# A three-stage kernel (decayed attention, routing, two expert layers): logits, scan resets, first routing step and tail rearranged

## The chip, the cores and the metric

One core of one Trainium2 chip runs the whole program. The metric is the device time of one execution in microseconds. Before the change the median of three runs is 825.63 us (824.81 to 825.66). The engines are TensorE (PE, with its weight loads as PEld), VectorE (DVE), ScalarE (ACT), GpSimd (POOL) and SyncE (SP, here the main issuer of DMA). They run side by side and wait for each other through semaphores.

## The reference

```python
# 1: attention with a decaying state, B=4, H=8, S=768, D=48
f = 1.0 / (1.0 + np.exp(-f_logit))
for t in range(S):
    state = f[:, :, t, :, None] * state + np.einsum('bhd,bhe->bhde', k[:, :, t], v[:, :, t])
    y[:, :, t] = np.einsum('bhd,bhde->bhe', q[:, :, t], state)
# 2: y as x (3072 tokens x 384); each token goes to one of 8 experts, 384 tokens each:
#    all (token, expert) pairs by falling logit; a pair is taken if the token is free
#    and the expert not full
logits = x @ w_gate
out[mask] = np.maximum(x[mask] @ w1[e], 0.0) @ w2[e]
# 3: on the result, rows scaled by rms and rms_g
g = xn @ w_gate2
y = (g / (1 + np.exp(-g)) * (xn @ w_val)) @ w_out
```

## The kernel before

**Attention** (`attention`, lines 322 to 596). Sixteen units, each a batch and a pair of heads; four units make a batch. A unit's 768 positions are cut in 6 chunks of 128. For a unit, `decays` (L403) lets ScalarE make `G`, the sigmoid of the forget logits. `scans` (L424) resets `G` at each chunk's first position by a memset of a very large number on VectorE (L427), and then runs one scan forward (`P`, L428) and one back (`W`, L431). With `one`, a constant in PSUM, as the second operand, the reset starts the running product anew. `kt` (VectorE) and `qt` (GpSimd) are keys and queries times these. TensorE turns the keys (`k_back`, L455), makes the products of a chunk with itself (`inner`, L469) and the chunk sums `U` (L483), which VectorE scans into states `st` (L487). Two units later `values` (L503) makes the outputs into two PSUM banks, and ScalarE copies them to `YT` (L509; for the last unit VectorE copies one half). The units are written out in one order by the loop `for i in range(-1, NU + 2)`, with no scheduler behind it: each engine takes its instructions in written order.

**Logits.** After a batch's last `values`, `logits` (L515) multiplies `YT` with the gate weights, in four strips of the TensorE array, 32 output partitions each, one strip a pair of heads, for each half `g` of the positions. ScalarE copies the result out (`lgT`, L518). A little later `logits_turn` (L522) multiplies each 128 positions by `sel`, which adds the four strips up and turns them: six products of 8 columns a batch. ScalarE copies them to `lg` (L525).

**Routing** (`Route`, lines 79 to 260; `slots`, L273). While the last units run, VectorE takes the range of the first 18 of 24 blocks of 128 tokens (`range`, L113) and scales it (`start`, L127 to L180); this is `extra["edges"]` in the loop. Behind the last logits, `favourites` (L171) finds each token's best expert, `hits` (L75) compares its distance with 128 marks, and TensorE counts the tokens per mark and expert (`cnt`, L217). That is step 0; four more steps choose again among the open experts. Each step begins with some row blocks of `YT` that are turned back (`Rows.put`, L612), copied by ScalarE and stored to DRAM by SP (`Rows.take`, L621, L622). `slots` makes the list `idx` (L319), by which GpSimd gathers the rows for the experts (L842).

**Experts and the last layer.** Eight experts (L1088, L1089), then twelve chunks of the gated layer. At its end, behind the loop, the products of the last four of twelve blocks are made for the two outputs `O[0]` and `O[1]`, `finish` copies each (L1163), and GpSimd scatters it to DRAM (L1166).

Of the kernel before, what the change touches and what calls it, by code (L numbers as in the profile page):

```python
# [20 lines left out]
BIG = 1.0e30  # L21
# [49 lines left out]
def hits(nc, wk, name, marks, x, g, G):  # L71

    c = wk.tile([128, G // 4, 128, 4], BF, name=f"{name}{g}", bufs=1)
# [7 lines left out]
class Route:  # L81
# [9 lines left out]
    def __init__(self, tc, K, lg, A, ident, pmin, pool):  # L91
# [5 lines left out]
        self.m0 = pool.tile([128, NB], F32, name="m0")  # L97
        self.v = pool.tile([128, 3], F32, name="v")
# [8 lines left out]
        self.n = 0  # L107
# [59 lines left out]
    def favourites(self, oh, d):  # L167

        nc, NB, E, n = self.tc.nc, self.NB, self.E, self.n
        if n < NB:  # L170
            nc.vector.tensor_reduce(out=self.m0[:, n:], in_=self.lg[:, n:], axis=AX.X, op=OP.max)  # L171
        nc.vector.tensor_scalar(d, self.m0, self.gm[:, 2:3], self.s0, op0=OP.add, op1=OP.mult)
        nc.vector.tensor_tensor(out=oh, in0=self.lg, in1=self.m0[:, :, None].to_broadcast([128, NB, E]),
                                op=OP.is_equal)
# [8 lines left out]
    def steps(self, n, Tp, rows=None, side=None):  # L183
# [5 lines left out]
        with self.tc.tile_pool(name="r_wk", bufs=2) as wk, self.tc.tile_pool(name="r_ps", bufs=1, space=PSUM) as ps:  # L189
# [8 lines left out]
            def one(s):  # L198
                oh = wk.tile([128, NB, E], BF, name="oh")
                d = wk.tile([128, NB], BF, name="d")  # L200

                if rows:
                    for n in ((4,), (3, 2), (3, 2), (4,), (4,))[s]:
                        rows.put(n)
                        rows.take(n)
                    side(s)
# [5 lines left out]
                else:  # L212
                    self.favourites(oh, d)
                cnt = ps.tile([128, E], F32, name="cnt")
# [23 lines left out]
    def run(self, n, flag, idx, ident, rows=None, side=None, more=None):  # L238
# [4 lines left out]
        def check(wk, ps, cum):  # L243
# [4 lines left out]
            ct = ps.tile([128, E + 2], F32, name="ct")  # L248
# [25 lines left out]
def slots(tc, K, A, ident, idx, check=None):  # L274
# [3 lines left out]
    with tc.tile_pool(name="s_wk", bufs=1) as wk, tc.tile_pool(name="s_ps", bufs=1, space=PSUM) as ps:  # L278
# [30 lines left out]
        for g in range(0, NB, 8):  # L309
            hots.update(hits(nc, wk, "ro", K["io"], r, g, 8))  # L310
# [10 lines left out]

def attention(tc, fT, kT, qT, vL, YT, w_gate, lg, pmin, ident, gcol, rms_g, extra):

# [15 lines left out]

    NR = 3  # L340
# [32 lines left out]
    one = psl.tile([128, 1], F32, name="one")  # L373
# [6 lines left out]
    lgp = [t[:, 384:408].rearrange("p (n e) -> p n e", e=8) for t in YP]  # L380
    sel = cst.tile([128, 8], F32, name="sel")
# [4 lines left out]
    nc.vector.tensor_reduce(out=sel, in_=ident.rearrange("q (p e) -> q e p", p=NP)[:, 0:8, :], axis=AX.X, op=OP.add)  # L386
# [877 lines left out]
```

## Time and profile before

| what | us |
|---|---|
| median of the runs | 825.63 |
| the profiled execution, its own time | 826.22 |
| its span, first to last instruction | 824.5 |
| TensorE waits for `kt` of VectorE | at 15.58 (0.88) and 26.70 (0.69) |
| before the half-clock stretch from 28.8 | `values`, that wait, `k_back`, products of a unit |
| before the one from 49.3 | products of a unit, `U` sums (48 columns), a turn (8 columns) |
| one turn of logits, to the next product | 1.43 (95.20 to 96.63) |
| one row block turned back by TensorE | 0.42 (2.08 for 5, from 119.46) |
| one product into a last output | 0.18 (24 records from 812.75 to 817.08) |
| `idx` written, gathers start | 141.0, 142.2 |

The times are microseconds from the first instruction. A product of fp32 operands is two records of TensorE, and records overlap, so a group's mean duration is longer than its share of the busy time. The profiled execution is one of its own; its time is 0.6 us above the median of the runs.

### The profile page before, as it was taken

The numbers are of one execution on the slowest core, as the hardware profiler recorded it, in microseconds if no ns is written. First come the engines' busy times: TensorE is split into PE (matmuls) and PEld (weight loads), VectorE is DVE, ScalarE is ACT, GpSimd is POOL, SyncE is SP. The second block draws the span as 40 slices with busy tenths as digits, with TensorE's granted clock in tenths as the row PEclk, the third lists the DMA queues.
The fourth block names the chain that finished last, engine by engine and source line by source line (L and its number), as shares of the span: only waits on it lengthen the run. The fifth ranks groups of instructions, "written<-read, shape, count | busy, mean of one in ns | idle before, by whom it ended". The sixth has DMA issues, their size and how long they took to land.

```text
span 824.5 us, 16903 instructions
## 1 busy us (share of the span) xinstructions
PE 796.4 (97%) x6745; PEld 770.6 (93%) x6745; DVE 484.7 (59%) x868; ACT 387.9 (47%) x844; POOL 276.1 (33%) x328
## 2 busy tenths in 40 slices
PE   7999986999999999999999999999999999999996
PEld 7888875899999999999999999999999999999996
DVE  8999867778988988465443434434344434344322
ACT  5777653455554564675344342425343343424221
POOL 7878701277777787150201011010202010110100
PEclk9999997999999999999999999999999999999999
DMA  9997155877787779341000000000000000000000
GB/s 275 233 230 203 31 173 216 267 264 245 241 306 253 253 238 314 116 147 39 20 2 20 1 20 2 20 1 20 19 3 20 2 20 2 20 1 20 2 20 20
DMA packets 44246, 88.59 MB, mean 107 GB/s; under 512 B 5856, under 2 KB 23520, under 8 KB 44160
## 3 DMA queue, kind: packets, MB, share of 16 engines
q1 hardware_dynamic: 35088, 70.90, 27.7%
q0 software_dynamic: 3072, 9.44, 3.3%
q10 hardware_dynamic: 6000, 7.09, 2.5%
q8 instruction: 55, 0.90, 0.5%
q14 instruction: 31, 0.25, 0.1%
HBM read 70.90 MB, written 16.52 MB: 106 GB/s over the span
## 4 chain that ended last, share of the span: by engine, by line
PE 61%; issue 8%; DVE 8%; DMA 2%; ACT 2%; POOL 1%; ACTq 0%; DVEq 0%; POOLq 0%
PE o L630 5%; PE o L628 5%; PE o L629 5%; PE g L628 5%; PE g L630 5%; PE g L629 5%; PE v L630 5%; PE v L629 5%; PE v L628 5%; PE x L629 3%; PE x L630 2%; PE x L628 2%; DVE w L819 2%; PE h L629 2%; DVE nb L1012 2%
## 5 line engine op out<-in xcount | busy, mean ns | idle before, releaser
L1188 DVE TENSOR_TENSOR hf<-sg,v 128x256 f32<-128x256 f32 x144 | 59.9, 416 | 165.0 <-PE v L630 115.2
L950 POOL TENSOR_TENSOR xlo<-xn,xhi 128x256 fp32r<-128x256 f32 x36 | 29.4, 820 | 312.2 <-ACT xhi L949 312.2
L1191 ACT CAST hh<-hf 128x256 fp32r<-128x256 f32 x144 | 58.6, 407 | 132.4 <-DVE hf L1188 132.4
L630 PE MATMUL g<-xhi,w 128*128 128x256 f32 x432 | 119.3, 276 | 0.0
L628 PE MATMUL g<-xhi,w 128*128 128x256 f32 x432 | 119.3, 276 | 0.0
L629 PE MATMUL g<-xlo,w 128*128 128x256 f32 x432 | 119.3, 276 | 0.0
L630 PE MATMUL v<-xhi,w 128*128 128x256 f32 x432 | 119.3, 276 | 0.0
L628 PE MATMUL v<-xhi,w 128*128 128x256 f32 x432 | 119.2, 276 | 0.0
L629 PE MATMUL v<-xlo,w 128*128 128x256 f32 x432 | 119.2, 276 | 0.0
L1192 DVE TENSOR_TENSOR hl<-hf,hh 128x256 fp32r<-128x256 f32 x144 | 61.2, 425 | 68.1 <-ACT hh L1191 67.6
L630 PE MATMUL o<-w,hl 128*128 128x384 f32 x288 | 98.6, 342 | 0.0
L628 PE MATMUL o<-w,hh 128*128 128x384 f32 x288 | 97.4, 338 | 0.2 <-ACT hh L1191 0.2
L629 PE MATMUL o<-w,hh 128*128 128x384 f32 x288 | 97.1, 337 | 0.0
L1186 ACT ACTIVATE sg<-g 128x256 f32<-128x256 f32 x144 | 55.3, 384 | 88.2 <-PE g L630 87.9
L628 PEld LDWEIGHTS g<-xhi,w 128*128 128x128 f32 x432 | 81.1, 188 | 0.0
L629 PEld LDWEIGHTS v<-xlo,w 128*128 128x128 f32 x432 | 81.1, 188 | 0.0
L628 PEld LDWEIGHTS v<-xhi,w 128*128 128x128 f32 x432 | 81.1, 188 | 0.0
L630 PEld LDWEIGHTS v<-xhi,w 128*128 128x128 f32 x432 | 81.1, 188 | 0.0
L630 PEld LDWEIGHTS g<-xhi,w 128*128 128x128 f32 x432 | 81.1, 188 | 0.0
L629 PEld LDWEIGHTS g<-xlo,w 128*128 128x128 f32 x432 | 81.0, 188 | 0.0
L1015 POOL TENSOR_TENSOR nr<-nr,ne 128x384 f32<-128x384 f32 x36 | 61.4, 1705 | 43.2 <-DVE ne L1014 12.9
L629 PE MATMUL x<-hl,w 128*128 128x384 f32 x192 | 65.7, 342 | 3.4 <-DVE hl L1089 3.3
(237 smaller groups left out, 1880.8 us busy)
## 6 DMA issues: line engine op xcount, KB each, us to landing
wraw<-in_moe_w_dram SPq DMA_DIRECT2D x32, 768.0 KB, 7.7
v<-in_v_rows_dram SPq DMA_DIRECT2D x16, 288.0 KB, 4.7
x_dram<-xrows SPq DMA_DIRECT2D x24, 192.0 KB, 5.7
nraw<-in_moe_w_gate_dram SPq DMA_DIRECT2D x12, 384.0 KB, 4.6
nraw<-in_moe_w_val_dram SPq DMA_DIRECT2D x12, 384.0 KB, 3.9
nraw<-in_moe_w_out_dram SPq DMA_DIRECT2D x12, 384.0 KB, 4.1
raw_f<-in_f_logit_turned_dram SPq DMA_DIRECT2D x26, 144.0 KB, 5.4
raw_k<-in_k_turned_dram SPq DMA_DIRECT2D x26, 144.0 KB, 4.1
```

What stands on the lines that cost most here:

```text
L628: nc.tensor.matmul(out, lhs[0], rhs[0], start=first, stop=False)
L629: nc.tensor.matmul(out, lhs[0], rhs[1], start=False, stop=False)
L630: nc.tensor.matmul(out, lhs[1], rhs[0], start=False, stop=last)
L819: eng.tensor_tensor(out=lo, in0=raw, in1=hi.bitcast(F32), op=OP.subtract)
L950: eng.tensor_tensor(out=lo, in0=s, in1=hi.bitcast(F32), op=OP.subtract)
L1012: nc.vector.scalar_tensor_tensor(out=b, in0=hw, scalar=-0x40000000, in1=b, op0=OP.bitwise_and, op1=OP.bitwise_or)
L1015: nc.gpsimd.tensor_tensor(out=r, in0=r, in1=e2.bitcast(F32), op=OP.mult)
L1186: nc.scalar.activation(sg, pg, AF.Silu)
L1188: nc.vector.tensor_tensor(out=h, in0=sg, in1=pv, op=OP.mult)
L1191: nc.scalar.copy(hh, h)
L1192: nc.vector.tensor_tensor(out=hl, in0=h, in1=hh.bitcast(F32), op=OP.subtract)
```

## The change

- *Logits.* One PSUM bank a batch instead of two. A strip now holds three pieces of 128 positions in two columns' places (256 columns), and the four pairs of heads are added in PSUM by four rounds of products into the same strips. `sel` has two forms and the turn is two products of 48 columns. `sel` is now filled by ScalarE.
- *Scan resets.* A ScalarE copy of `big` behind the sigmoid replaces VectorE's memset, for all units but the first.
- *Early favourites.* For the first 16 blocks, favourites and comparisons are made ahead, behind `start`; they are counted by TensorE between the last logits and their turn. Step 0 has 8 blocks left. The counts, `one` and a check's sums lie in a PSUM bank of their own (`bank0`), and the comparisons in one fixed buffer (`cm`).
- *Order.* The memset of the banks for the last `values` stands before `start`; a minimum over `pall` stands later. Row blocks by step: 1, 2, 5, 5, 5, 6 instead of 2, 4, 5, 5, 4, 4 (the first number is ahead of the steps).
- *End.* The products for the last two outputs stand in another order, and the second output is copied in two halves, by ScalarE and VectorE.

```diff
+    def early(self, pool, cnt):
+        nc, NB, E = self.tc.nc, self.NB, self.E
+        n = self.ready = 16
+        self.cnt = cnt
+        self.oh0 = pool.tile([128, NB, E], BF, name="oh0")
+        self.d0 = pool.tile([128, NB], BF, name="d0")
+        self.favourites(self.oh0, self.d0, 0, n)
+        self.hot = {}
+        self.compare(0, 12)
+    def compare(self, g, G):
+        self.hot.update(hits(self.tc.nc, self.cm, "cm", self.K["io"], self.d0, g, G))
+    def count(self):
+        for i, c in self.hot.items():
+            self.tc.nc.tensor.matmul(self.cnt, c, self.oh0[:, i], start=(i == 0), stop=False)
...
-                    for n in ((4,), (3, 2), (3, 2), (4,), (4,))[s]:
+                    for n in ((2,), (3, 2), (3, 2), (3, 2), (3, 3))[s]:
...
-                for g, G in self.PARTS:
-                    for i, c in hits(nc, wk, "cm", K["ed"] if s else K["io"], d, g, G).items():
+                for g, G in ((16, 8),) if ahead else self.PARTS:
+                    for i, c in hits(nc, self.cm, "cm", K["ed"] if s else K["io"], d, g, G).items():
...
             nc.scalar.activation(G[i][:, t], raw("f", i)[:, t], AF.Sigmoid)
+        if i:
+            nc.scalar.copy(G[i][:, 0:S:C], big)
...
-        nc.vector.memset(g[:, 0:S:C], BIG * 1.0e8)
...
-    def logits(b, g):
-        o = bank()
-        for p in range(NP):
-            nc.tensor.matmul(o[32 * p:32 * p + 32], wgp[g][0:112, p], YT[0:112, b, p, 384 * g:384 * g + 384],
-                             start=True, stop=True)
+    def logits(b):
+        o = bank()[:, 0:256]
+        for k in range(NP):
+            for r in range(4):
+                g, odd = divmod(r, 2)
+                p = (2, 0, 1, 3)[k] if odd else k
+                both = (p > 1) if odd else (p < 2)
+                a = 0 if both else 128 * odd
+                t = 384 * g + 128 * odd + a
+                w = 256 if both else 128
+                nc.tensor.matmul(o[32 * r:32 * r + 32, a:a + w], wgp[g][0:112, p], YT[0:112, b, p, t:t + w],
+                                 start=k == 0, stop=k == NP - 1)
...
-    def logits_turn(b, g):
-        for n in range(3):
-            nc.tensor.matmul(lgp[g][:, n, :], LG[b, g][:, n * 128:n * 128 + 128], sel, start=True, stop=True)
+    def logits_turn(b):
+        for n in range(2):
+            nc.tensor.matmul(lgp, LG[b][:, n * 128:n * 128 + 128], sel[:, n], start=n == 0, stop=n == 1)
...
             if i == NU + 1:
-                for g in range(2):
-                    logits_turn(units[i - 2][0], g)
-                    logits_sum(units[i - 2][0], g)
-        if i == NU - 1:
-            extra["edges"](bank())
-        load("fkq", i + 4)
+                extra["rest"]()
+            logits(units[i - 2][0])
+            if i == NU + 1:
+                extra["count"]()
+                logits_turn(units[i - 2][0])
+                logits_sum(units[i - 2][0])
         if i == NU - 1:
             for _ in range(2):
                 YL.append(bank())
                 nc.vector.memset(YL[-1][32:64], 0.0)
-        if i == NU:
+            extra["edges"](bank())
+        load("fkq", i + 4)
+        if i == NU + 1:
             nc.vector.tensor_reduce(out=pmin, in_=pall.rearrange("p a b -> p (a b)"), axis=AX.X, op=OP.min)
...
-                (nc.scalar.copy if m % 2 else nc.vector.tensor_copy)(t, O[m])
+                if c == NCH - 1 and m:
+                    nc.scalar.copy(t[:, 0:DM // 2], O[m][:, 0:DM // 2])
+                    nc.vector.tensor_copy(t[:, DM // 2:], O[m][:, DM // 2:])
+                else:
+                    (nc.scalar.copy if m % 2 else nc.vector.tensor_copy)(t, O[m])
...
+        held = [(0, KG - 4), (0, KG - 3), (0, KG - 2), (1, KG - 4), (0, KG - 1), (1, KG - 3), (1, KG - 2), (1, KG - 1)]
```

*TensorE, between the last unit's `values` and the first count of the routing.* Before: `bank<-at,v` and `bank<-qt,st` are the last `values`, then both halves' logits, their turns (`lgT`), six row blocks of four products, and the count.

```order
L503 MATMUL bank<-qt,st 48x128 x10
L515 MATMUL bank<-YT,wgp_127 32x384 x4
L515 MATMUL bank<-YT,wgp_128 32x384 x4
L522 MATMUL yp_131<-sel,lgT 128x8 x3
L522 MATMUL yp_132<-sel,lgT 128x8 x3
L612 MATMUL rows<-ident,YT 128x112 x24
L217 LDWEIGHTS cm_2054
L217 MATMUL cnt<-oh,cm_2054 128x8
```

Changed, the logits of a batch (the same 12 rows stand for every batch), and then the end of the early counts, the turn, three row blocks and the counts that are left:

```order
L544 MATMUL bank<-YT,wgp_132 32x256 x2
L544 MATMUL bank<-YT,wgp_133 32x256 x2
L544 MATMUL bank<-YT,wgp_132 32x256
L544 MATMUL bank<-YT,wgp_132 32x128
L544 MATMUL bank<-YT,wgp_133 32x256
L544 MATMUL bank<-YT,wgp_133 32x128
L544 MATMUL bank<-YT,wgp_132 32x128 x2
L544 MATMUL bank<-YT,wgp_133 32x128 x2
L544 MATMUL bank<-YT,wgp_132 32x128
L544 MATMUL bank<-YT,wgp_132 32x256
L544 MATMUL bank<-YT,wgp_133 32x128
L544 MATMUL bank<-YT,wgp_133 32x256
```

```order
L126 LDWEIGHTS cm
L126 MATMUL bank_92<-oh_1896,cm 128x8
L551 MATMUL yp_136<-sel,lgT 128x48 x2
L644 MATMUL rows<-ident,YT 128x112 x12
L237 LDWEIGHTS cm
L237 MATMUL bank_92<-oh_1896,cm 128x8
```

Eight products of 384 columns are now sixteen of 256 or 128, six turns are two, and 16 of the 24 counts stand ahead of the turn.

*VectorE, at the end of the attention.* `far` is the last instruction of `start`, `m` the best logit of each token, `d` its distance, `oh` its expert, `cm` the comparisons. Before:

```order
L180 TENSOR_SCALAR far<-down,sc,off 128x144
L593 MEMSET bank 32x384 x2
L595 TENSOR_REDUCE pmin<-pall 128x1
L509 COPY YT<-bank 112x384
L192 MEMSET ok 128x4
L171 TENSOR_REDUCE m_1821<-lg 128x6
L172 TENSOR_SCALAR d<-m_1821,gm,s_1826 128x24
L173 TENSOR_TENSOR oh<-lg,m_1821 128x192
L75 TENSOR_TENSOR cm_2054<-iota_173,d 128x1536
L75 TENSOR_TENSOR cm_2068<-iota_173,d 128x1024
L75 TENSOR_TENSOR cm_2078<-iota_173,d 128x512
```

Changed, first where the last unit's `st` is made, then from `far` on:

```order
L495 TENSOR_TENSOR at<-bank,mask 128x384 x2
L509 SCALAR_TENSOR_TENSOR st<-U,z_144 128x288
L623 MEMSET bank 32x384 x2
L146 TENSOR_REDUCE gm<-bank 128x3
L147 TENSOR_SCALAR range<-gm 128x1
```

```order
L199 TENSOR_SCALAR far<-down,sc,off 128x144
L191 TENSOR_SCALAR d_1897<-m_1828,gm,s_1834 128x16
L192 TENSOR_TENSOR oh_1896<-lg,m_1828 128x128
L75 TENSOR_TENSOR cm<-iota_177,d_1897 128x1536
L531 COPY YT<-bank 112x384
L75 TENSOR_TENSOR cm<-iota_177,d_1897 128x512
L627 TENSOR_REDUCE pmin<-pall 128x1
L211 MEMSET ok 128x4
L190 TENSOR_REDUCE m_1828<-lg 128x6
L191 TENSOR_SCALAR d_1897<-m_1828,gm,s_1834 128x8
L192 TENSOR_TENSOR oh_1896<-lg,m_1828 128x64
L75 TENSOR_TENSOR cm<-iota_177,d_1897 128x1024
```

The two memsets of `bank` have moved from behind `far` to ahead of `gm`; the comparisons of 12 and 4 blocks now stand on either side of the copy of `YT`, and behind the reduction of the last 6 blocks one comparison of 8 blocks is left.

*VectorE, at the end of the program, with what each instruction waits for.* Before:

```order
L1188 TENSOR_TENSOR hf<-sg,v 128x256 [waits PE_49,Activation_49]
L1192 TENSOR_TENSOR hl_10861<-hf,hh_10860 128x256 [waits Activation_49]
L1188 TENSOR_TENSOR hf<-sg,v 128x256 [waits PE_49,Activation_49]
L1192 TENSOR_TENSOR hl_10889<-hf,hh_10888 128x256 [waits Activation_49]
L1163 COPY ot<-o_10492 128x384 [waits DMASW6_49,DMASW3_49,PE_49]
```

Changed:

```order
L1234 TENSOR_TENSOR hl_10839<-hf,hh_10838 128x256 [waits Activation_49]
L1230 TENSOR_TENSOR hf<-sg,v 128x256 [waits PE_49,Activation_49]
L1234 TENSOR_TENSOR hl_10867<-hf,hh_10866 128x256 [waits Activation_49]
L1205 COPY ot<-o_10470 128x384 [waits DMASW6_49,DMASW3_49,PE_49]
L1203 COPY ot<-o_10471 128x192 [waits DMASW7_49,Activation_49]
```

The first output's copy stands as before; behind it stands half of the second output's copy, with a wait for ScalarE.

## Rows read from the trace of the kernel before

**Rows 1.** stretches in us, busy us of PE, PEld, DVE, ACT, POOL, clock, DMA share, GB/s
```profile
28.80:32.20 3.40, 3.40 (x46) 3.15 (x44) 3.30 (x5) 2.52 (x7) 2.97 (x4) 0.51 1.07 246
...
49.30:52.70 3.40, 3.40 (x42) 3.01 (x41) 3.23 (x5) 0.00 (x0) 1.46 (x4) 0.50 1.02 242
52.70:97.00 44.30, 44.18 (x811) 37.74 (x807) 41.19 (x45) 35.15 (x102) 37.01 (x55) 1.00 0.59 152
...
134.60:144.90 10.30, 7.31 (x48) 6.79 (x49) 5.44 (x19) 0.14 (x1) 3.50 (x4) 0.50 0.11 32
```

**Rows 2.** waits from 12 to 97 us: total, times, longest
```profile
PE bank L455 <- DVE kt L440: 1.6, 2, 0.9
DVE st L487 <- ACT at L475: 1.3, 2, 1.1
```

**Rows 3.** VectorE where `idx` is written
```profile
141.02 0.18 DVE L319 TENSOR_TENSOR idx<-t 128x24 int32<-128x24 f32 x1
```

**Rows 4.** TensorE in order of time, the count of the third routing step
```profile
122.31 1.23 PE L217 MATMUL cnt<-oh,cm 128*128 128x8 bf16 x24 [0.34 <-DVE cm L75]
```

**Rows 5.** TensorE's groups of one line and shape, 41 to 97 us
```profile
L522 PE MATMUL yp<-sel,lgT 128*128 128x8 f32 x36 | 4.5, 258 | 0.0
L515 PE MATMUL bank<-YT,wgp 112*32 112x384 f32 x48 | 4.5, 492 | 0.0
```

**Rows 6.** VectorE in order of time, one unit and the last `kt`: start, duration
```profile
85.49 0.06 DVE L427 MEMSET G<- 128x6 f32 x1
85.67 1.75 DVE L428 TENSOR_TENSOR_SCAN P<-G,one 128x768 f32<-128x768 f32 x1
...
91.12 0.06 DVE L427 MEMSET G<- 128x6 f32 x1
...
95.10 1.03 DVE L440 TENSOR_TENSOR kt<-raw_k,W 128x768 f32<-128x768 f32 x1
```

**Rows 7.** TensorE in order of time, last units, last logits and last turn
```profile
92.44 0.51 PE L455 MATMUL bank<-ident,kt 48*128 48x48 f32 x10
...
98.92 0.51 PE L455 MATMUL bank<-ident,kt 48*128 48x48 f32 x10
...
105.47 1.52 PE L503 MATMUL bank<-at,v 128*48 128x128 f32 x24 [0.79 <-DVE bank L593]
...
107.76 1.89 PE L515 MATMUL bank<-YT,wgp 112*32 112x384 f32 x16
109.58 1.53 PE L522 MATMUL yp<-sel,lgT 128*128 128x8 f32 x12
```

**Rows 8.** VectorE in order of time, end of the attention and first routing step
```profile
102.64 0.53 DVE L127 TENSOR_REDUCE gm<-bank 128x3 f32<-128x384 f32 x1
...
104.95 0.78 DVE L593 MEMSET bank<- 32x384 f32 x2
...
107.88 0.56 DVE L509 COPY YT<-bank 112x384 f32<-112x384 f32 x1 [2.05 <-PE bank L503]
...
111.36 0.20 DVE L171 TENSOR_REDUCE m<-lg 128x6 f32<-128x48 f32 x1 [2.91 <-ACT lg L525]
...
112.08 1.90 DVE L75 TENSOR_TENSOR cm<-iota,d 128x1536 bf16<-128x1536 bf16 x3
```

**Rows 9.** VectorE's comparisons of the first routing step, by shape
```profile
L75 DVE TENSOR_TENSOR cm<-iota,d 128x1536 bf16<-128x1536 bf16 x1 | 1.0, 955 | 0.0
L75 DVE TENSOR_TENSOR cm<-iota,d 128x1024 bf16<-128x1024 bf16 x1 | 0.7, 684 | 0.0
```

**Rows 10.** the last eight stores of rows on SP's queue
```profile
126.18 7.47 SPq L622 DMA_DIRECT2D x_dram<-xrows  x8
```

**Rows 11.** ScalarE at the end
```profile
817.12 0.48 ACT L1163 COPY ot<-o 128x384 f32<-128x384 f32 x1 [3.24 <-PE o L630]
```

**Rows 12.** GpSimd's last two scatters
```profile
817.43 0.96 POOL L1166 DMA_INDIRECT out_dram<-ot,idx  x1 [32.77 <-DVE ot L1163]
...
818.70 0.96 POOL L1166 DMA_INDIRECT out_dram<-ot,idx  x1 [0.21 <-issue]
```

More of the change, by code (lines that the diff above doesn't have):

```diff
@@ L198, in one @@
             def one(s):
-                oh = wk.tile([128, NB, E], BF, name="oh")
-                d = wk.tile([128, NB], BF, name="d")
+                ahead = self.ready if rows and not s else 0
+                oh = self.oh0 if ahead else wk.tile([128, NB, E], BF, name="oh")
+                d = self.d0 if ahead else wk.tile([128, NB], BF, name="d")
                 if rows:
-                    for n in ((4,), (3, 2), (3, 2), (4,), (4,))[s]:
+                    for n in ((2,), (3, 2), (3, 2), (3, 2), (3, 3))[s]:
                         rows.put(n)
@@ L338, in attention @@
     psl = pool("a_psl", 1, space=PSUM)
+    big = cst.tile([128, NC], F32, name="big")
+    nc.gpsimd.memset(big, BIG * 1.0e8)
+    one = bank0[:, 0:1]
     NR = 3
@@ L379, in attention @@
     YP = [psl.tile([128, 512], F32, name=f"yp{i}") for i in range(2)]
-    lgp = [t[:, 384:408].rearrange("p (n e) -> p n e", e=8) for t in YP]
-    sel = cst.tile([128, 8], F32, name="sel")
+    lgp = YP[0][:, 384:432].rearrange("p (n e) -> p n e", e=8)
+    sel = cst.tile([128, 2, 2, 3, 8], F32, name="sel")
     for t in YP:
@@ L544, in attention @@
                                   w_gate.rearrange("(p h d) e -> h d p e", h=2, d=D)[h])
+            nc.gpsimd.memset(sel, 0.0)
+            rows = ident.rearrange("q (g r e) -> q g r e", g=2, r=2)
+            for n in range(2):
+                nc.scalar.copy(sel[:, n, :, n:n + 2], rows[:, :, :, 0:8])
         if i - 1 in extra:
@@ L788, in prepare, with edges @@
         R.append(Route(tc, K, lg, A, ident, pmin, ytp))
+        R[0].ct = bank0[:, 16:26]
         R[0].range(18)
+    def edges(bank):
+        R[0].start(bank)
+        R[0].early(ytp, bank0[:, 8:16])
     def consts(bank):
@@ L797, in tile_kernel @@
     YT = ytp.tile([128, 4, 4, NT // 4], F32, name="YT")
+    bank0 = yt.enter_context(tc.tile_pool(name="ps0", bufs=1, space=PSUM)).tile([128, 512], F32, name="bank0")
     ctx.enter_context(tc.manual_schedule())
-    attention(tc, fT, kT, qT, vL, YT, w_gate, lg, pmin, ident, gcol, rms_g,
+    attention(tc, fT, kT, qT, vL, YT, w_gate, lg, pmin, ident, gcol, rms_g, bank0,
               {-2: consts, 1: lambda bank: turn_inc(tc, K, bank[:, 0:128], ident), "range": prepare,
-               "edges": lambda bank: R[0].start(bank)})
+               "edges": edges, "rest": lambda: R[0].compare(12, 4), "count": lambda: R[0].count()})
     wpool = ctx.enter_context(tc.tile_pool(name="w", bufs=16))
@@ L862, in tile_kernel @@
             rows = Rows(tc, YT, x_dram, ident, rw, rwp)
-            rows.put(2)
-            rows.take(2)
+            rows.put(1)
+            rows.take(1)
             R = R[0]
```

59 lines of the change are left out of this document (26 added, 33 removed).

## The prediction

> **What bounds the kernel now.** I read the busy shares by stretch first. From 52.7 to 97 us TensorE is busy 44.18 of 44.30 us, VectorE 41.19, GpSimd 37.01, ScalarE 35.15 [rows 1]. So the attention is TensorE's, with VectorE close behind. The list of waits agrees: TensorE waited for `kt` of VectorE only twice, 1.6 us in all (at 15.6 and 26.7, in the small table above the change), and VectorE waited once worth naming, 1.3 us for ScalarE [rows 2]. Two stretches of 3.4 us, at 28.8 and at 49.3, ran at a granted clock of 0.51 and 0.50, the lower of the two levels [rows 1]. Before the first TensorE had stood waiting for VectorE; before the second it ran `U` sums and the turn, products of 48 and 8 columns.
>
> Behind the attention, one chain runs through all engines until `idx` is written at 141.0 [rows 3]. VectorE sets its pace, and TensorE waits for it in the steps (0.34 us in a step with five rows) [rows 4]. From 145 us on TensorE is full again to the end. The change touches nothing there but the last outputs. A microsecond won before `idx` is therefore a microsecond of the kernel, if nothing takes its place.
>
> **The change part by part.** A unit is one pair of heads, 16 in all.
>
> *Turns.* Three batches are turned inside TensorE's full stretch: 36 records, 4.5 us busy, 1.5 a batch [rows 5]. A product of this type is two records, and of six products two stay, so 8 of 12 records go: 1.0 us. Columns rise from 8 to 48, which the records' 258 ns, mostly weight load and drain, should not feel. I take 0.9, since the change of tile shape at both ends stays: 3 x 0.9 = -2.8 (bounds -2.0 and -3.0).
>
> *Logits.* 48 records took 4.5 us, though one takes 492 ns: 16 x 0.492 = 7.9 us of work in 1.5, so the strips run beside each other [rows 5]. A strip has 768 columns, before (2 x 384) and after (256 + 256 + 128 + 128). In written order a wide product stands beside a narrow one in the second and fourth round; if each round waits for its widest, a strip counts 256 + 256 + 128 + 256 = 896, and 1.5 x 896/768 is 0.25 more. Between 0 and 0.25 I take 0.1: three batches, +0.3.
>
> *Scan resets.* The memset costs VectorE 0.18 us a unit (85.49 to the scan at 85.67) of 5.63 (to 91.12) [rows 6]. It is on the path only while TensorE waits for `kt`: the units up to the first half-clock stretch, 4 x 0.18, taken as -0.5 (bounds 0 and -0.7). ScalarE's new copy of 6 elements has its cover in the 9 us that ScalarE is free of 44.3; the scan that reads it comes a unit later. Without that cover, at the 0.18 us that VectorE pays for the same elements, it would cost 15 x 0.18 = 2.7 us.
>
> *The half-clock stretches.* Each costs half of 3.4, 1.7 us. With the turn cut to a third the second has less that is narrow ahead of it; with VectorE still slower than TensorE in the first units (5.4 us against 6.48 less a turn of 1.43, about 5.05 [rows 6, 7]) the first can come again. I take one of the two as gone: -1.7 (bounds 0 and -3.4; a third one would add 1.7).
> The Trainium skill (TensorE: Matmul & The Clock Gate, What's actually happening) says that the clock's monitor looks in a rhythm of its own that does not start with the kernel. By that rule the stretches move from run to run, and the sum is anything from 0 to -3.4 in each; the one trace here can't tell.
>
> Does VectorE let TensorE run ahead? The last unit's `kt` starts at 95.10 and ends near 96.1, and TensorE reads it at 98.92 [rows 6, 7]. VectorE loses 14 x 0.18 and its wait of 1.3, so `kt` is ready by 92.3; TensorE at -4.7 reads it at 94.2. VectorE is the cap at -6.6 and is late next. Attention: -2.8 + 0.3 - 0.5 - 1.7 = -4.7.
>
> *Memset of the last banks.* TensorE stood 0.79 us before 105.47 for them [rows 7]. They now stand ahead of the range's arithmetic, 0.78 for the two [rows 8]: -0.8. Behind them on VectorE waits that arithmetic (102.64 to 104.8), now with favourites (about 0.5) and the comparison of 12 blocks (0.96) in front of the copy of `YT` [rows 8, 9]: 102.64 + 0.78 + 2.2 + 0.5 + 0.96 = 107.1. TensorE now delivers at 107.88 - 0.79 = 107.09, so this copy is just not late: 0 (bounds 0 and +0.5).
>
> *Last logits and turn.* From 107.76 to the reduction at 111.36 it is 3.6 us [rows 7, 8]. After: logits 1.6; one evacuation that no second half hides, 0.5 estimated from the gap to the turn; turn 1.53 x 4/12 = 0.5; copy and hand-over 0.5: 3.1. The 16 early counts fit the wait for the evacuation (24 of them took 1.23 [rows 4], so 0.8): -0.5 (bounds 0 and -0.9).
>
> *Favourites and comparisons.* On the path stand 1.90 us for 24 blocks [rows 8]; 8 blocks at 0.68 remain [rows 9]: -1.2. The early parts stand in idle time of VectorE, 2.05 before its `YT` copy and 2.91 before the reduction [rows 8]. If TensorE were late with the counts, half would go: bounds -0.6 and -1.2.
>
> *Rows.* Three instead of six stand ahead of the first count, and six, not four, in the last step. The step with five rows left TensorE 0.34 us before its count [rows 4]; a row is about 0.4 (the table), so with six it is late by 0.1. Their stores: SP issues the last eight from 126.18 over 7.47 us, and DMA is 0.11 busy after 134.6 [rows 1, 10], while `idx` comes at 141.02 [rows 3]. Two rows more at the end and a chain shorter by 1.2 leave some 4 us. I take 0 (bounds 0 and +1.5, the latter if the copies of the last rows wait for buffers that DMA still reads).
>
> *End.* The first scatter holds GpSimd from 817.43, so the second starts at 818.70, although its copy ended at 817.60 [rows 11, 12]. Now nine more records follow the first output instead of three, six at 0.18 (the table) earlier, 1.1 us, where 0.6 is enough. The second output is copied in halves, and VectorE's half waits for ScalarE's: 0.3 and 0.38, estimates from 0.48 for the whole on ScalarE, after 817.12, and 0.25 to GpSimd's start (0.21 stood before the second scatter): 818.05, -0.6.
> The Trainium skill (PSUM — Partial Sum Buffer, PSUM bank collisions raise a hardware error) forbids two engines the same bank and partitions at once, and the wait in the changed order is what that demands. By it the halves run one after the other and the sum has -0.6; side by side they would give -0.9, and one undivided copy, 817.60 + 0.25, gives -0.8. The rule speaks against the split, not against the reordering.
>
> Sum: -4.7 - 0.8 - 0.5 - 1.2 - 0.6 = -7.8. The profiled execution took 826.22 us (span 824.5 and 1.7 around it), so 818.4; the median of the runs is 0.6 lower, so 817.8.
>
> **The rivals.**
> (a) *The clock takes its share.* Both stretches come again, or one moves into the routing, where fewer rows stand between narrow products. For: nothing in the first units changes but 0.18 us of 5.6. Against: the second stood behind a turn that shrinks. -7.8 + 1.7 = -6.1: 819.5.
> (b) *Both stretches go.* TensorE comes near the cap: -9.5, 816.1.
> (c) *The routing gives its part back.* The pile of rows in the last steps or VectorE's late `YT` copy eats the gain of the favourites and of the last turn: -7.8 + 1.7 + 0.8 = -5.3, 820.3. For: the `YT` copy has no margin. Against: the slack to `idx`.
> (d) *Slower: the strips no longer run beside each other.* The four rounds now add into one bank with unequal widths. If a product of one strip waited for the one before it in another, a block would take up to 4 x 1.5 = 6 us, +4.5 each, four times +18: 825.6 - 7.8 + 18 = 835.8. It decides from a block of 1.5 + 7.8/4 = 3.5 us. Against: before, too, four strips wrote one bank.
> (e) *The turns' gain is not there*, as VectorE or ScalarE paces the attention once TensorE is lighter: -7.8 + 2.8 = -5.0, 820.6. Against: 1.9 us of margin at the last `kt`.
>
> **How the numbers follow.** Forecast 0.42; (a) 0.22; (b) 0.12; (c) 0.08; (e) 0.08; (d) 0.04; something unseen that eats all of it 0.04. The forecast's own range, from its bounds without the clock, is 816.6 to 819.3. The range to hold eight in ten takes in (a), (b), (c) and (e) and a microsecond for the run: 815.2 to 822.0. A difference under 0.2%, 1.65 us, can't be told from none. Faster holds all cases but (d) and the unseen, less a little for both (c) and (e) together: 0.91; same 0.04; slower 0.05.
>
> **What would show it.** Three turns of about 0.5 us and logits of 1.5 to 1.75; no VectorE memset between `st` and the scan; the last banks' values with no wait on a memset; the first reduction of the last six blocks some 3.1 us after the logits' start, one comparison behind it; `idx` near 133.8; the second scatter about 1.0 us after the copy's start. Wrong would be: logits over 2 us, `kt` waits in TensorE after 34 us worth more than a microsecond, steps over 4.5 us, or three half-clock stretches before 100 us.

## The result and the profile after

The changed kernel takes 817.79 us, the median of four executions (816.55 to 819.74), beside 825.64 of the kernel before: ratio 0.9906, 95% interval 0.9882 to 0.9929. Six more executions later gave 817.63 and 0.9918 (0.9904 to 0.9933). The forecast was 817.8. The profiled execution is the slowest of the four, 819.74 with a span of 818.0; its gain is 6.5 us of span, and the traces below account for that.

Busy time, clock and DMA by stretch, in the columns of [rows 1]:

```profile
9.90:16.70 6.80, 6.25 (x53) 5.67 (x50) 6.70 (x7) 4.10 (x16) 5.00 (x8) 0.50 0.97 301
16.70:97.00 80.30, 80.29 (x1546) 70.35 (x1545) 74.92 (x77) 65.50 (x193) 67.50 (x103) 1.00 0.90 191
139.60:143.00 3.40, 3.31 (x14) 2.74 (x15) 1.11 (x4) 0.92 (x3) 1.93 (x3) 0.50 0.62 204
```

Both half-clock stretches of the attention are gone; TensorE is busy 80.29 of 80.30 us and waits for no `kt` [rows 2]. But there is one in the start, at 9.9, where this profile of the kernel before had none, and another at 139.6, among the first products of the experts.

TensorE's groups from 41 to 97 us (the answer to [rows 5]), then TensorE in order of time from the last unit to the last logits [rows 7]:

```profile
L544 PE MATMUL bank<-YT,wgp 112*32 112x256 f32 x48 | 4.6, 387 | 0.0
L544 PE MATMUL bank<-YT,wgp 112*32 112x128 f32 x48 | 3.1, 272 | 0.0
L551 PE MATMUL yp<-sel,lgT 128*128 128x48 f32 x12 | 1.9, 284 | 0.0
```

```profile
94.26 0.51 PE L477 MATMUL bank<-ident,kt 48*128 48x48 f32 x10
...
99.89 1.52 PE L525 MATMUL bank<-at,v 128*48 128x128 f32 x24
101.34 0.91 PE L525 MATMUL bank<-qt,st 48*48 48x128 f32 x20
102.18 1.53 PE L544 MATMUL bank<-YT,wgp 112*32 112x256 f32 x32
103.64 0.69 PE L126 MATMUL bank<-oh,cm 128*128 128x8 bf16 x16
```

The turns have 12 records instead of 36. The logits have twice the records of before, the wide and the narrow ones, in nearly the same time: 1.46 us from the first of them to the next product (102.18 to 103.64), where before it was 1.43 (65.75 to 67.18). The strips still run beside each other, and unequal widths cost some 0.03 us. The last unit's `k_back` starts at 94.26 instead of 98.92; the last batch's `values` (99.89) follow with no wait.

VectorE in order of time: a unit, the end of the attention with the first routing step, and `idx` (the answers to [rows 6, 8, 9, 3]):

```profile
85.48 0.96 DVE L462 TENSOR_TENSOR kt<-raw_k,W 128x768 f32<-128x768 f32 x1
86.36 0.75 DVE L509 TENSOR_TENSOR_SCAN st<-U,z 128x288 f32<-128x288 f32 x1
87.02 1.73 DVE L450 TENSOR_TENSOR_SCAN P<-G,bank 128x768 f32<-128x768 f32 x1
...
90.80 1.02 DVE L462 TENSOR_TENSOR kt<-raw_k,W 128x768 f32<-128x768 f32 x1
```

```profile
98.14 0.78 DVE L623 MEMSET bank<- 32x384 f32 x2
...
102.30 0.56 DVE L531 COPY YT<-bank 112x384 f32<-112x384 f32 x1
...
105.10 0.20 DVE L190 TENSOR_REDUCE m<-lg 128x6 f32<-128x48 f32 x1 [1.74 <-ACT lg L554]
...
105.67 0.68 DVE L75 TENSOR_TENSOR cm<-iota,d 128x1024 bf16<-128x1024 bf16 x1
...
107.69 0.42 DVE L170 SCALAR_TENSOR_TENSOR open<-T,down 128x96 f32<-128x96 f32 x2 [0.52 <-PE T L215]
...
133.81 0.18 DVE L339 TENSOR_TENSOR idx<-t 128x24 int32<-128x24 f32 x1
```

No memset stands between `st` and the scan, and a unit takes VectorE 5.32 us (85.48 to 90.80). From the last logits to the reduction it is 2.92 us (102.18 to 105.10), before 3.60; from there to the first `open` 2.59, before 3.88. `idx` is written at 133.81, 7.21 us earlier.

The end, ScalarE, VectorE and GpSimd in turn [rows 11, 12]:

```profile
811.23 0.32 ACT L1202 COPY ot<-o 128x192 f32<-128x192 f32 x1 [3.23 <-PE o L662]
```

```profile
811.58 0.36 DVE L1203 COPY ot<-o 128x192 f32<-128x192 f32 x1 [1.36 <-ACT ot L1202]
```

```profile
812.22 0.96 POOL L1208 DMA_INDIRECT out_dram<-ot,idx  x1 [0.68 <-DVE ot L1203]
```

From the start of the last copy to the second scatter it is 0.99 us, before 1.58. The halves run one behind the other, as the wait shows.

Where the time went, in us by stage; "before 1" and "after 1" are the profiles discussed so far, the others those of E7, E11, E1 and E10 below. Each unit has one group of `U` products. Stages are bounded by TensorE's first and last `U` group, the last logits, the reduction behind them, the first and the last `open`, `idx` and the first `hl` of an expert:

| stage | before 1 | E7 | E11 | E1 | after 1 | E10 |
|---|---|---|---|---|---|---|
| to the first `U` | 11.39 | 12.34 | 12.31 | 11.61 | 12.95 | 11.79 |
| first to last `U` | 89.87 | 88.82 | 87.17 | 86.32 | 83.58 | 83.47 |
| to the last logits | 6.50 | 6.50 | 6.50 | 6.49 | 5.64 | 5.64 |
| to the reduction | 3.60 | 3.60 | 3.60 | 2.92 | 2.92 | 2.92 |
| to the first `open` | 3.88 | 3.88 | 3.87 | 3.88 | 2.59 | 2.59 |
| four steps | 17.68 | 17.67 | 18.03 | 17.68 | 18.01 | 17.90 |
| to `idx` | 8.10 | 8.10 | 8.09 | 8.10 | 8.11 | 8.03 |
| to the first `hl` | 12.41 | 12.03 | 12.24 | 12.23 | 13.24 | 12.16 |
| to the end | 671.08 | 671.51 | 671.06 | 671.25 | 670.98 | 670.62 |

In E11 the clock is at half from 126.2 to 129.6, in its third and fourth step; its 18.03 goes with that.

### The profile page after: what moved, and what is told of

The parts are those of the page before. It is cut to its first block, busy times and chain, and to the rows that moved or that the text cites. A ratio compares the mean times of both kernels' runs of the same rounds, so it can differ in the third digit from the quotient of the medians.

```text
span 818.0 us, 16930 instructions
## 1 busy us (share of the span) xinstructions
PE 793.5 (97%) x6777; PEld 769.6 (94%) x6777; DVE 483.6 (59%) x855; ACT 389.4 (48%) x853; POOL 275.4 (34%) x330
## 4 chain that ended last, share of the span: by engine, by line
PE 62%; issue 9%; DVE 8%; ACT 2%; DMA 1%; POOL 1%; POOLq 0%; ACTq 0%; DVEq 0%
PE o L662 5%; PE o L660 5%; PE o L661 5%; PE g L660 5%; PE g L662 5%; PE g L661 5%; PE v L662 5%; PE v L661 5%; PE v L660 5%; PE x L661 3%; PE x L662 3%; PE x L660 2%; PE h L661 2%; PE h L660 2%; PE h L662 2%
## 5 line engine op out<-in xcount | busy, mean ns | idle before, releaser
L1053 POOL TENSOR_TENSOR nr<-nr,ne 128x384 f32<-128x384 f32 x36 | 58.9, 1636 | 42.8 <-DVE ne L1052 14.5
```

Of the source, the lines that this page charges most:

```text
L1053: nc.gpsimd.tensor_tensor(out=r, in0=r, in1=e2.bitcast(F32), op=OP.mult)
```

## The experiments

**The attention: E1, only the logits; E2, only the resets.** E1 is the kernel before with the new logits, `sel` and turn; E2 with ScalarE's resets and nothing else:

```diff
+        if i:
+            nc.scalar.copy(G[i][:, 0:S:C], big)
...
-        nc.vector.memset(g[:, 0:S:C], BIG * 1.0e8)
```

> The kernel before with the new logits, turn and two selection products alone; memsets on VectorE, no favourites, old rows, old end. Theory (TensorE sets the pace of the attention once VectorE has got ahead, and a turn's products are what falls away): turns 0.6 us each instead of 1.43, logits unchanged at 1.45, so about -2.5 us in the attention before any change of the clock; in the tail -0.7 from the last logits' start to the reduction; the wait of 0.8 us for the last banks' memset and the second half-clock stretch may stay. Sum -3.2, with up to -1.7 more if the second half-clock stretch goes with the shorter turn: 821 to 822.5. Rival (VectorE paces the attention once TensorE is lighter): TensorE waits for kt by about 0.8 us a turn, k_back of the last unit at most 1 us earlier, sum -1.7. Rival (strips with unequal widths wait for each other): logits 1.7 us and more.

> The kernel before with ScalarE writing the scan's resets, and nothing else. Theory: VectorE's unit is 0.18 us shorter, but TensorE is waited on, so only the wait for kt in the first units shrinks: -0.3 to -0.7 us by itself. If the first half-clock stretch (at 28.8 in the kernel before) came from that wait, it goes too, another -1.7; then k_back of the last unit lies 2.0 to 2.4 earlier. Rival: VectorE's units add up behind the whole attention, -14 x 0.18 = -2.5 us without any change of the clock. Rival: the copy on ScalarE makes the scan late, as the changed kernel's two waits of 0.38 and 0.24 us for it hint: 0 or slower.

E1 took 822.82 us, ratio 0.9970 (0.9958 to 0.9982), -2.4 us by the medians; E2 824.11 us, 0.9988 (0.9975 to 1.0001), -1.1, which can't be told from none. Neither has a half-clock stretch between 20 and 100 us, so the attention's gain can't be read against the first profile of before; E11 serves for that. The logits and the last turn came as expected (3.60 to 2.92). But in E1 TensorE waits for VectorE's `kt`, and for ScalarE behind it. The list of waits of E1, then of the full change in a start of the same kind (E10), both from 12 to 97 us:

```profile
PE bank L454 <- DVE kt L439: 1.6, 3, 0.6
PE bank L468 <- ACT kn L456: 1.0, 4, 0.3
```

```profile
PE bank L491 <- ACT kn L479: 0.3, 1, 0.3
```

TensorE's `U` groups of the third and the sixth unit show where. First E1, with the first logits behind them, then E10, then the sixth of E2, and of E11, a profile of the kernel before:

```profile
23.51 0.66 PE L482 MATMUL U<-v,kn 128*48 128x48 f32 x20
...
41.17 0.66 PE L482 MATMUL U<-v,kn 128*48 128x48 f32 x20
41.76 0.62 PE L521 MATMUL bank<-YT,wgp 112*32 112x256 f32 x5
```

```profile
23.69 0.66 PE L505 MATMUL U<-v,kn 128*48 128x48 f32 x20
...
38.84 0.66 PE L505 MATMUL U<-v,kn 128*48 128x48 f32 x20
```

```profile
38.73 0.65 PE L486 MATMUL U<-v,kn 128*48 128x48 f32 x20
```

```profile
40.39 0.65 PE L483 MATMUL U<-v,kn 128*48 128x48 f32 x20
```

From the third to the sixth unit E1 takes 17.66 us and E10 15.15. These 2.51 us are most of the 2.85 that E1 is longer from first to last `U` (86.32 - 83.47). They lie ahead of the first logits, and so ahead of every turn: the shorter turns can't have made VectorE the bound there. A unit without logits or turn is 4.92 us of TensorE, and from `kt` to `kt` VectorE needs some 5.56 with the memset (E1) and 5.32 to 5.40 without (E10). So VectorE is the slower one in these units in any case, and TensorE waits for it unless VectorE has a lead from the start. In these profiles the lead goes with how long the clock is at half in the start (between 9 and 18 us):

| | before 1 | E7 | E11 | E1 | E2 | after 1 | E10 |
|---|---|---|---|---|---|---|---|
| resets by | VectorE | VectorE | VectorE | VectorE | ScalarE | ScalarE | ScalarE |
| turns | old | old | old | new | old | new | new |
| half clock in the start | none | 6.8 | 6.8 | 3.4 | none | 6.8 | 3.4 |
| sixth `U` at | 40.63 | 40.62 | 40.39 | 41.17 | 38.73 | 40.11 | 38.84 |
| sixth to last `U` | 60.63 | 60.54 | 59.10 | 56.76 | 59.11 | 56.43 | 56.42 |

With 6.8 us of half clock TensorE's second `U` comes at 19.8 to 20.2 instead of 17.4 to 18.4, and VectorE has its lead: there the resets give 0.28 and 0.51 us by the sixth `U` (E11 and E7 against after 1). In the other starts they give 1.90 (before 1 against E2) and 2.33 (E1 against E10; of this, 0.52 is one wait of VectorE for GpSimd at 33.73 in E1). Behind the sixth `U` they give nothing with the old turns (E11 against E2) and 0.34 with the new ones (E1 against E10). The new logits and turns give 2.69 there with the resets on ScalarE (E2 against E10) and 2.34 without (E11 against E1). So E1's rival, a VectorE that paces the lighter TensorE by 0.8 us a turn, is not borne out. Each of these is a pair of single profiles, and before 1 also has its stretch at 28.8 ahead of the sixth `U`.

**The half-clock stretches: E7 and E11, the kernel before, unchanged, profiled twice more.**

> The kernel before, unchanged, profiled a second time. Theory (the half-clock stretches of the attention belong to the moment and not to the code): they are not at 28.8 and 49.3 us again, but elsewhere, once or not at all, and the last unit's product lies up to 3.4 us earlier than 98.92. Rival (they belong to this kernel's narrow products and its wait for kt): both stand there again within a microsecond.

> The kernel before, unchanged, a third profile, for the half-clock stretches of the attention alone. Theory (the old turns, two unlike tile shapes and 36 records of 8 columns, bring the clock down now and then): one or two stretches of 3.4 us between 20 and 100 us again, at other places. Rival (pure chance, as the kernel with ScalarE's resets and the old turns had none): none here in the attention, and k_back of the last unit at 97 us or earlier.

E7 (826.15 us) has stretches from 10.9 and 72.4, E11 (824.59 us) one from 10.2 and none in the attention behind it. So a stretch in the start, as in the first profile after, comes without the change too. The windows of E7's two, and of E11's attention:

```profile
10.90:17.70 6.80, 6.80 (x51) 6.49 (x51) 6.59 (x7) 2.76 (x10) 4.35 (x7) 0.50 1.02 315
72.30:75.80 3.50, 3.50 (x44) 3.04 (x40) 3.32 (x5) 0.06 (x1) 1.20 (x3) 0.51 0.77 190
```

```profile
19.70:99.50 79.80, 79.24 (x1461) 67.90 (x1459) 73.60 (x87) 61.81 (x180) 65.49 (x98) 1.00 0.76 183
```

So the same program has none, one or two of them, at other places each time. That agrees with the Trainium skill (TensorE: Matmul & The Clock Gate, What's actually happening), which has the monitor's rhythm start apart from the kernel. Behind the sixth `U` E7, with one, takes 1.44 us more than E11, and before 1, with that at 49.3, 1.53 more: somewhat less than the half of 3.4 that one stretch was taken to cost. The one at 28.8 cost nothing to be seen: the sixth `U` of before 1 is at 40.63, and at 41.17 in E1, where none stands there but TensorE waits for `kt`. Of the eleven profiles of other code, ten have none that begins between 17 and 100 us (E2 with its old turns among them); E8 has one from 18.9. Whether the long turns make a stretch likelier (two of three profiles of before have at least one) is not settled by so few.

**E10, the changed kernel again.**

> The changed kernel again, for more executions and a second profile. Theory: 817.8 within 1 us; no half-clock stretch between the first three units and the last logits (six traces with the short turn have none, apart from the one with the short idle loop; two of before have two and one). If the loss of 0.8 us between idx and the first hl came from the half-clock stretch that stood at 139.6 in the first profile, first xhi is here 6.7 to 7.1 behind idx (7.69 there) and first hl 5.2 to 5.3 behind that (5.56 there). Rival: the loss comes with the change, and 7.7 and 5.56 stand again.

It took 817.63 us, a profiled span of 815.1. Behind the start no stretch stands in the attention, nor one among the experts. From `idx` to the first `hl` it is 12.16 us, and 11.92 to 12.39 in the seven other profiles of the changed kernel's variants, where none begins between the two. So the 13.24 of the first profile, 0.83 more than before 1, came with its stretch at 139.6 and not with the change.

**E8, a shorter idle loop in the start.** TensorE keeps itself busy with products of no use behind the first unit (`spin`).

```diff
-                spin(nc, bank()[:, 0:128], ident, 11)
+                spin(nc, bank()[:, 0:128], ident, 4)
```

> The changed kernel with 4 products instead of 11 in the idle loop of TensorE behind the first unit. Theory (in the changed kernel this loop, at half clock, ends at 17.8 us and so holds the second unit, whose kt VectorE has ready at 15.1): the second unit starts 2.0 to 2.7 us earlier, of which 1.5 to 1.9 remain at the last unit, where VectorE's kt (91.8 us) is the cap; time -1 to -1.9 us. Where the clock does not fall in the start, 0 to -0.3. Rival (the loop is needed): with TensorE idle for 2 us the clock falls again behind it and the attention loses 1.7 us or more, so that the time is no better.

818.55 us, 0.9921 (0.9903 to 0.9938): no better than the change. TensorE in order of time, first of the changed kernel, then of E8:

```profile
13.93 4.05 PE L291 MATMUL bank<-ident 128*128 128x128 f32 x22
17.91 0.52 PE L477 MATMUL bank<-ident,kt 48*128 48x48 f32 x10
...
23.13 0.51 PE L477 MATMUL bank<-ident,kt 48*128 48x48 f32 x10
```

```profile
14.97 0.72 PE L477 MATMUL bank<-ident,kt 48*128 48x48 f32 x10
...
18.73 0.94 PE L505 MATMUL U<-v,kn 128*48 128x48 f32 x20 [0.95 <-DMA v<-in_v_rows_dram]
...
23.41 0.51 PE L477 MATMUL bank<-ident,kt 48*128 48x48 f32 x10
```

The second unit starts 2.9 us earlier, more than expected, but the third no earlier (23.41 against 23.13): TensorE waits for `v`, which is still being loaded, and its clock falls again at 18.9. My theory fell, and the rival's mark is there. Part of the 2.9 us is not the loop's: E8 has 3.4 us of half clock in the start and the first profile after 6.8. In E10, with 3.4 and the long loop, the second unit starts at 16.30 and the third at 21.51, so E8's third is later than that by 1.9. Whether the shorter loop made the clock fall again, one profile can't tell.

**The routing: E3, no early favourites; E4, other row counts.**

```diff
-        R[0].early(ytp, bank0[:, 8:16])
...
-               "edges": edges, "rest": lambda: R[0].compare(12, 4), "count": lambda: R[0].count()})
+               "edges": edges, "rest": lambda: None, "count": lambda: None})
```

```diff
-                    for n in ((2,), (3, 2), (3, 2), (3, 2), (3, 3))[s]:
+                    for n in ((3,), (3, 2), (3, 2), (3, 2), (3, 2))[s]:
```

> The changed kernel without early favourites: all comparisons and counts of the first step stand behind the last reduction again. Theory: from the reduction to the first open, 2.59 us becomes 3.9 (+1.2 to +1.3), idx later by that; the last turn and reduction 0 to 0.2 earlier, since no counts stand in front of them. Rival (the early work only moved the wait, TensorE being late with the counts): 3.2 or less.

> The changed kernel with 3, 5, 5, 5, 5 instead of 2, 5, 5, 5, 6 rows in the steps (the order of all rows unchanged). Theory (six rows do not fit in a step, and TensorE comes late to the count): the last step 4.42 us instead of 4.75, -0.33, and the first step no longer, as TensorE has room before the first count: idx 0.3 earlier. Rival (the last step is long for another reason, such as the copies that wait for buffers being stored): it stays at 4.7; or the row moved to the front makes the first step 0.3 to 0.4 longer and nothing is won.

One execution each, 818.64 and 819.09 us; the stages tell more. In E3 the reduction lies 2.92 us behind the last logits, and the first `open` 3.87 behind it:

```profile
104.13 0.20 DVE L190 TENSOR_REDUCE m<-lg 128x6 f32<-128x48 f32 x1 [2.07 <-ACT lg L554]
...
108.00 0.42 DVE L170 SCALAR_TENSOR_TENSOR open<-T,down 128x96 f32<-128x96 f32 x2 [0.57 <-PE T L215]
```

Early favourites are worth 3.87 - 2.59 = 1.28 us, and the counts ahead of the turn cost nothing. E4 went against its theory: the steps took 4.42, 4.42, 5.07 and 4.70 us, where the change has 4.42 three times and 4.75. It is not the sixth row as such; E3, with six rows and a last step that begins 1.2 us later, has 4.42 in its last step (its first step, 5.28, has the clock at half from 108.3 to 111.7). In the changed kernel ScalarE and then TensorE, in order of time:

```profile
120.70 0.48 ACT L653 COPY xrows<-rows 128x384 f32<-128x384 f32 x1 [2.11 <-DMA x_dram<-xrows]
121.07 1.48 ACT L914 CAST w<-wraw 128x1536 fp32r<-128x1536 f32 x1
122.45 1.62 ACT L653 COPY xrows<-rows 128x384 f32<-128x384 f32 x4
```

```profile
120.75 1.70 PE L644 MATMUL rows<-ident,YT 112*128 112x112 f32 x16
122.98 0.99 PE L644 MATMUL rows<-ident,YT 112*128 112x112 f32 x8 [0.54 <-ACT xrows L653]
```

ScalarE stands 2.11 us before a copy whose buffer is still being stored, then converts weights for 1.48 us, and TensorE runs out of banks.

**E6, the last load of weights behind the rows; E9, that with an undivided last copy; E12, the conversions late too.** The core of the edit of E6 and E9; E12 calls `side(6)` too:

```diff
-                if s < 3:
-                    w_load(0, s + 1)
-                if 0 < s < 5:
+                if s < 2 or s == 4:
+                    w_load(0, min(s + 1, 3))
+                if 0 < s < 4 or s == 5:
...
             R.run(5, flag, idx, ident, rows, side)
+            side(5)
```

> The changed kernel with the fourth load of weights (768 KB) moved from the third step of the routing behind the last rows, and its conversion on ScalarE behind the steps. Theory (the last step is longer, 4.75 us instead of 4.42, because ScalarE's copies of rows wait for buffers whose stores share a full DMA with these weights, and TensorE then waits for a bank): some 1.9 us of transfer (768 KB at 395 GB/s) no longer lie in front of the last rows, so all four later steps take 4.42 us, and the wait of TensorE for the copies (0.54 us) is gone. Rival (six rows are simply too many for one step): the last step stays at 4.7.

> The changed kernel with the fourth load of weights behind the last rows and the last output copied undivided. Theory: -0.33 us from the last step and -0.26 at the end, together about -0.6 against the changed kernel: 817.2 where that stands at 817.8, ratio to the kernel before 0.990. In the trace four steps of 4.42 us and a second scatter 0.75 us after the start of its copy. Rival (what is won before idx is lost among the experts, as the late weights hold up the first expert): first hl later by the same 0.3 behind idx, and no difference in time.

> The kernel with late weights and the undivided last copy, and the conversions of the third and fourth part of the weights (1.48 us each on ScalarE) both behind the last step, where ScalarE is free until idx. Theory (in the last step ScalarE waits for a buffer whose store lands late, and then the 1.48 us of conversion stand in its queue ahead of the six copies; in the version before that made 5.31 us of the last step): the copies begin 1.5 us earlier, and all four steps are 4.42 us in any moment of the DMA; idx 0.3 to 0.9 earlier than with the conversion ahead; time -0.6 against the changed kernel, 817.1. Rival (the store that lands late is enough by itself): the last step stays at 4.6 or more. Rival (the conversions hold up the first expert): first xhi over 7.1 us behind idx.

E6 took 817.05 us in its one execution, with steps of 4.42, 4.42, 4.42 and 4.44, as hoped; E9, the same there, 817.75 us, 0.9912 (0.9900 to 0.9925), with a last step of 5.31. ScalarE in E6 and in E9:

```profile
120.18 0.48 ACT L653 COPY xrows<-rows 128x384 f32<-128x384 f32 x1 [1.80 <-DMA x_dram<-xrows]
120.56 1.48 ACT L915 CAST w<-wraw 128x1536 fp32r<-128x1536 f32 x1
```

```profile
121.60 0.48 ACT L653 COPY xrows<-rows 128x384 f32<-128x384 f32 x1 [2.02 <-DMA x_dram<-xrows]
121.98 1.48 ACT L915 CAST w<-wraw 128x1536 fp32r<-128x1536 f32 x1
```

The step begins at 120.74 in E6 and at 121.30 in E9: counted from there, the copy that waited for the store is 0.86 us later in E9, and the step is 0.87 longer. E12, 817.58 us and 0.9904 (0.9885 to 0.9923), has its last step at 4.42, but the second at 4.97 and the third at 5.16, the third with the clock at 0.71. In the second step ScalarE stood before its conversion of weights:

```profile
113.15 1.47 ACT L915 CAST w<-wraw 128x1536 fp32r<-128x1536 f32 x1 [2.68 <-DVE m L173]
```

The same conversion starts at 111.70 in the changed kernel. The line names VectorE, but the load of these weights, issued at 106.72, has its last of sixteen parts landing at 112.97 in this trace, one part 1.5 us behind the others (111.46), and at 111.53 in the changed kernel. The row copies start behind it, at 114.53, and TensorE waits 1.06 us for them. So a transfer that lands late behind a full DMA is the cause, a store of rows in the last step of the change and of E9, a load in the second step of E12; moving weights or conversions only moves the step that meets it. None of the three is measurably faster than the change.

**E5, two parts undone.** The last banks' memset stands behind the range's arithmetic again, and the last output is copied undivided.

```diff
+            extra["edges"](bank())
             for _ in range(2):
...
-            extra["edges"](bank())
...
-                if c == NCH - 1 and m:
-                    nc.scalar.copy(t[:, 0:DM // 2], O[m][:, 0:DM // 2])
-                    nc.vector.tensor_copy(t[:, DM // 2:], O[m][:, DM // 2:])
-                else:
-                    (nc.scalar.copy if m % 2 else nc.vector.tensor_copy)(t, O[m])
+                (nc.scalar.copy if m % 2 else nc.vector.tensor_copy)(t, O[m])
```

> The changed kernel with two parts undone that lie far apart in time: the memset of the last banks stands behind the range's arithmetic again, and the last output is copied undivided. Theory: TensorE waits some 0.8 us for VectorE before the first values of the last batch (the changed kernel has no such wait), the arithmetic of the range is no use in being 0.8 earlier; and at the end the undivided copy takes 0.48 us on ScalarE, so that the second scatter starts 0.73 us after the start of that copy instead of 0.99: the split costs 0.26 us. Rival for the first: VectorE, which now runs ahead of TensorE, has the memsets done in time in either order, 0. Rival for the end: the split is hidden behind the first scatter (1.5 us before the second), 0.

One execution, 821.02 us; its clock is also at half from 102.3 to 105.7, in the last `values` and logits, so its time is not used. TensorE's wait, VectorE's memset, and at the end ScalarE's copy and GpSimd's second scatter:

```profile
PE bank L525 <- DVE bank L624: 2.1, 1, 2.1
```

```profile
101.17 0.79 DVE L624 MEMSET bank<- 32x384 f32 x2
```

```profile
812.75 0.48 ACT L1201 COPY ot<-o 128x384 f32<-128x384 f32 x1 [3.24 <-PE o L662]
```

```profile
813.51 0.96 POOL L1204 DMA_INDIRECT out_dram<-ot,idx  x1 [0.45 <-ACT ot L1201]
```

TensorE waits 2.1 us, not 0.8: the memset now stands behind the early favourites too, which the theory had left out. At the end the undivided copy has the scatter 0.76 us behind its start instead of 0.99: the split costs 0.23 us.

## Why the prediction was right, and where it was not

The time came out as forecast, and most terms did. The sum also owes something to errors that cancel.

- *Turns*, -2.8: right. From `U` to `U` across a turn 6.65 became 5.73 us in E11 and E10, three times 0.92.
- *Logits*, +0.3: nearly nothing came of it. The strips lose nothing to speak of by unequal widths (+0.03 a batch between `U` groups, 6.48 to 6.51); rival (d) is out.
- *Scan resets*, -0.5 with bounds 0 and -0.7: right in its place, the units in which TensorE waits for `kt`, but mis-sized. There the resets give 0.3 to 0.5 us, or 1.90, or 2.33, by the start that the execution has. The 0.18 us a unit was near (VectorE's unit fell by 0.16 to 0.24), but single waits went with it, and the term didn't ask whether VectorE has a lead from the start. In the medians E2 shows -1.1, with an interval from -2.1 to +0.1. Behind the sixth unit the term is nothing, as predicted, or 0.34 beside the new turns.
- *Half-clock stretches*, -1.7, "one of the two as gone": mis-sized and without a cause. They belong to the execution: of three profiles of before one has both, one has one, one has none. Of the two in the first profile, that at 49.3 cost 1.53 us and that at 28.8 nothing to be seen, as TensorE would have waited for `kt` there. In the first profile after both were gone but one in the start came instead, which held the second unit's `k_back` to 17.91 (15.58 before).
- *The attention's sum*, -4.7: the last unit's `k_back` went from 98.92 to 94.26, -4.66. The agreement is partly luck. -0.52 arose up to the sixth `U`, where the start took back most of what the resets gave. Of the rest about 2.7 are the logits and turns, and 1.5 the stretch at 49.3, which not every execution of before has. Between profiles with the same 6.8 us of half clock in the start and none behind it, E11 and after 1, the last `U` moved by 2.95 us, from 99.49 to 96.54. With E2's -1.1 for the resets and nothing for the stretches, the measured terms add up to -6.9, which is what the medians of E10 and of the kernel before beside it gave (817.63 and 824.52); the first four executions gave -7.85. What the stretches are worth in a median was not measured.
- *VectorE as the cap at -6.6*: it did not come to that. Its last `kt` ends at 91.82, 2.4 us before TensorE reads it, and in E1, with the memsets, still 1.05 before.
- *Last banks' memset*, -0.8: -0.86. As predicted, VectorE's `YT` copy (102.30) was just not late: it starts as the last product of `values` ends (102.25).
- *Last logits and turn*, -0.5: -0.68, mostly the turn. *Favourites*, -1.2: -1.29 here, 1.28 in E3.
- *Rows*, 0 with a bound of +1.5 "if the copies of the last rows wait for buffers that DMA still reads": that is what happened, at +0.33 (+0.22 in E10). The last step of 4.75 us is also one of the prediction's own signs of being wrong (steps over 4.5). Rival (c) was right in its mechanism and small in size.
- *End*, -0.6: -0.59. The undivided copy would give 0.23 more, near the 0.2 that the sum for it allowed.
- *Rivals* (a) and (b) each had a part of it: a stretch came in the start, and both in the attention went. Rival (e) is out: even with the memsets (E1) the new logits and turns kept 2.34 us behind the sixth unit, of 2.69 with the resets on ScalarE.
- *The range* from its bounds, 816.6 to 819.3, has about all the lower bounds in it but only one of the upper ones, +1.5 for the rows; with all of them it would reach some 822.6. And the 1.3 us for which VectorE waited for ScalarE were two waits, the longer 1.1 [rows 2].
- *Not foreseen*: 0.83 us more from `idx` to the first `hl` in the first profile. E10, with 12.16 against 12.0 to 12.4 before, shows that it goes with the stretch of half clock there.

## What to carry to other kernels

Price an edit on an engine that nearly paces by stage, and not by the mean over a batch: here a quarter of a microsecond of VectorE a unit counted in the units ahead of the first logits, where TensorE needs 4.92 us a unit and VectorE over 5.3, and hardly behind them; and it counted only in executions whose start gives VectorE no lead. When two profiles that differ by one edit differ in time, look where, before a reason is given: here most of the difference lay ahead of the first turn. Take a second profile of the kernel before ahead of putting a price on low-clock stretches. Where a chain that shares its time with DMA gets shorter, look for the copies whose buffers are still being stored; they are met a little earlier with each microsecond won.

## What the runs showed of the hardware

Sixteen logits products in four strips, eight of 256 and eight of 128 columns, adding in PSUM, take 1.46 us a batch; before, eight of 384 columns took 1.5 [rows 5]. And a stretch of half clock costs by what stands there. One of 3.4 us where TensorE is full cost 1.44 and 1.53 us (E7 and before 1 against E11); one where TensorE would have waited for VectorE cost nothing to be seen. In the start, the two profiles of the changed kernel differ by 3.4 us of it before the second unit; their sixth `U` groups then differ by 1.27 us (40.11 and 38.84) and their last by 1.28 (96.54 and 95.26). The nine profiles of the changed kernel and its variants take 56.39 to 56.43 us from the sixth to the last `U`, whatever their start.
